# Attention in front of two expert layers: query parts stacked on the partitions, two score products per head instead of three

## The chip, the cores and the metric

The kernel runs on one core of a Trainium2 chip as a single program. The metric is the device time of that program in microseconds, from launch to the last output; of several runs the median counts. The engines of the core have their own in-order instruction streams: TensorE (PE, with its weight loads shown apart as PEld), VectorE (DVE), ScalarE (ACT), GpSimd (POOL) and SyncE (SP, which here only issues DMAs).

## The reference

Attention over 4 sequences of 576 tokens, 8 heads of 64 elements, causal with a window of 128 and a linear bias per head, in float32. Its output (2304 tokens by 512) then goes through two layers of 8 experts each. Only the attention is touched here.

```python
scores = scale * np.matmul(q, k.transpose(0, 1, 3, 2))
mask = (rel >= 0) & (rel < window)                    # rel = i - j, window = 128
scores = np.where(mask, scores + bias[None], -1000000000.0)
attn = np.exp(scores - np.max(scores, axis=-1, keepdims=True))
attn = attn / (np.sum(attn, axis=-1, keepdims=True) + 1e-09)
attn_out = np.matmul(attn, v)
x = attn_out.transpose(0, 2, 1, 3).reshape(B * S, H * D)
x = _moe_ref(x=x, **moe_kwargs)
return _moe2_ref(x=x, **moe2_kwargs)
```

## The kernel before, in words

**Blocks and units.** A sequence is cut into four blocks of 128 tokens and a tail of 64 (`NB` = 4, `TL` = 64). The 4 sequences give 20 blocks. A block is worked off in four units, one for each pair of heads (`hp`). A unit computes the scores of 128 queries of both heads against the keys of the block and of the block before it (`qk`: 256 columns a head), adds the bias and finds the row minimum on DVE (L196), takes the exponent on ACT (L200), turns the result on PE (`trans`), copies it back to SBUF on ACT and DVE (L229 to L233), and multiplies it with v on PE (`pv`, L255). The loop at the end of the attention keeps `trans` two units and `pv` four units behind `qk`. At `hp` 1 and 3 it prepares the keys and the queries of the block after next (`prep_k`, `prep_q`): four PE transposes each into one of two shared PSUM tiles `pT`, and from there to SBUF.

**The score product.** PE multiplies in a rounded 32-bit format (`F32R`). To keep float32 accuracy, q and k are each split into a high part (what ACT's copy rounds to) and a low part (what DVE's subtraction leaves). A unit's score of one head is the sum of three products: qh·kh, ql·kh, qh·kl (L193, L194). The two heads of a pair lie on partitions 0 to 63 and 64 to 127 of the key tiles `kt`; the query tiles `qt` hold zeros on the partitions of the other head, which are written once at the start (`clear_qt`, L111 on ACT, L115 on POOL). The first block of each sequence is computed in plain float32 (`qf`, `kf`, L190), which PE issues as two passes; the tail block has both heads of a pair in one product (L209, three products in F32R).

**What sets the order.** The Python loop gives the program order; a scheduler of the framework then places the instructions of each engine, and semaphores are put where tiles meet. The SP queue issues the loads (L72) about three blocks ahead and the writes of finished rows (`x_dram<-xr`, L313) in one in-order stream. POOL makes the distance table `rel` (L87 to L90) from which DVE makes the eight bias tables `bm` (L119), ahead of the first scores. After the attention the routing of the first expert layer begins, which needs the gate values of all tokens.

## Time and profile before

| | us |
|---|---|
| median of 3 runs (1073.11, 1077.97, 1077.48) | 1077.48 |
| the profiled execution | 1077.98 |
| its span, first to last instruction | 1076.1 |
| TensorE busy over the span | 947.7 (88%) |
| VectorE busy | 590.5 (55%) |
| ScalarE busy | 387.8 (36%) |
| GpSimd busy | 331.6 (31%) |
| mean granted TensorE clock | 0.93 |

The profiled execution is 1.9 us longer than its span and 0.5 us longer than the median of the runs. Busy shares over the whole span mix the attention (the first 180 us or so), the routing between the layers, and the expert products. For this change only the attention's stretch matters, and in it the views by time window and the timeline. PE's instructions overlap, so the duration shown of one matmul is longer than the step from one to the next; the step is read from the starts of the weight loads.

### The profile page before, as it was taken

The page shows a single profiled execution, that of the slowest core. Times are in us where ns is not written, and L with a number is a line of the kernel's source. Part 1 is how long each engine was busy: PE and PEld are TensorE (multiplying, and loading weights), DVE is VectorE, ACT ScalarE, POOL GpSimd, SP SyncE. Part 2 cuts the span into 40 slices and gives each one's busy share as a digit, 9 for nine tenths or more (in the row PEclk, how much of TensorE's full clock was granted, in tenths as well). Part 3 has the DMA queues.
Part 4 walks back from the last instruction along what each step waited for, and adds up shares of the span by engine and source line. Part 5 has one row for each costly group of instructions (what it writes and reads, how often), then busy time and mean ns, then how long its engine had stood idle before and what let it go on. Part 6 is the DMA issues. An engine that isn't in the chain of part 4 may idle for free. (4 is left out here: it accounts for less than half of the span.)

```text
span 1076.1 us, 18169 instructions
## 1 busy us (share of the span) xinstructions
PE 947.7 (88%) x6625; PEld 851.7 (79%) x6626; DVE 590.5 (55%) x1842; ACT 387.8 (36%) x793; POOL 331.6 (31%) x449
## 2 busy tenths in 40 slices
PE   8999998699999999989689698795995986959995
PEld 7999997488888799988579587685885886858894
DVE  8777686776797796878327153351531533515320
ACT  7777773223243264545115032221321322213210
POOL 9524421111100111032454417146153171461102
PEclk9999998599999999999799699898996998989998
DMA  9869621465443455545136144162351441623202
GB/s 203 204 145 211 162 66 55 149 206 170 148 154 108 125 168 167 179 122 181 46 59 186 35 108 134 46 137 76 89 132 30 108 133 46 134 79 90 32 11 35
DMA packets 114748, 125.66 MB, mean 117 GB/s; under 512 B 68128, under 2 KB 77344, under 8 KB 114656
## 3 DMA queue, kind: packets, MB, share of 16 engines
q1 hardware_dynamic: 98384, 90.93, 29.4%
q0 software_dynamic: 16272, 33.54, 14.6%
q8 instruction: 53, 0.87, 0.3%
q14 instruction: 39, 0.32, 0.1%
HBM read 100.69 MB, written 24.53 MB: 116 GB/s over the span
## 5 line engine op out<-in xcount | busy, mean ns | idle before, releaser
L899 PE MATMUL psG<-xh,w 128*128 128x312 f32 (+3 forms) x1536 | 362.0, 321 | 80.6 <-DVE hl L923 42.0
L899 PEld LDWEIGHTS psG<-xh,w 128*128 128x128 f32 x1536 | 273.4, 201 | 90.2 <-DVE hl L923 47.9
L899 PE MATMUL psG<-xl,w 128*128 128x312 f32 (+3 forms) x768 | 243.8, 318 | 3.3 <-issue 3.3
L923 DVE SCALAR_TENSOR_TENSOR hl<-psG,hh 128x312 fp32r<-128x312 f32 (+3 forms) x160 | 74.7, 475 | 247.4 <-ACT hh L922 169.9
L1334 PE MATMUL psG<-w,hh 128*128 128x512 f32 (+1 forms) x640 | 204.2, 396 | 0.1
L1224 POOL DMA_INDIRECT xrow<-x_dram,sr x156 | 153.2, 982 | 139.2 <-DVE sz L1041 63.2
L922 ACT ACTIVATE hh<-psG 128x312 fp32r<-128x312 f32 (+3 forms) x160 | 66.6, 426 | 307.3 <-PE psG L899 178.1
L899 PEld LDWEIGHTS psG<-xl,w 128*128 128x128 f32 x768 | 154.8, 202 | 3.0 <-issue 2.4
L1367 POOL DMA_INDIRECT out_dram<-y,sx x40 | 68.1, 1702 | 279.2 <-DVE y L1366 277.9
L1334 PEld LDWEIGHTS psG<-w,hh 128*128 128x128 f32 (+1 forms) x640 | 118.6, 185 | 30.5 <-DVE hl L923 0.6
L767 DVE TENSOR_TENSOR w<-raw,w 128x1024 fp32r<-128x1024 f32 x108 | 129.9, 1214 | 20.4 <-ACT w L766 17.2
L766 ACT ACTIVATE w<-raw 128x1024 fp32r<-128x1024 f32 x108 | 110.2, 1054 | 78.4 <-PE psG L1334 70.0
L1334 PE MATMUL psG<-w,hl 128*128 128x512 f32 (+1 forms) x320 | 126.4, 395 | 0.0
L749 POOL DMA_INDIRECT xg<-x_dram,ix x24 | 25.8, 1075 | 193.9 <-DVE w L426 54.1
L956 PE MATMUL psG<-hf,w2f 128*128 128x288 f32 x256 | 73.0, 426 | 0.0
L1366 DVE TENSOR_SCALAR y<-psG,sw 128x512 f32<-128x512 f32 (+1 forms) x40 | 29.7, 743 | 76.1 <-PE psG L1334 75.0
L1334 PEld LDWEIGHTS psG<-w,hl 128*128 128x128 f32 (+1 forms) x320 | 59.4, 185 | 14.6
L960 PE MATMUL psG<-hh,w 128*128 128x288 f32 x256 | 56.1, 305 | 3.9 <-ACT hh L922 3.9
L255 PE MATMUL pO<-v,pt 128*128 128x65 f32 x448 | 58.8, 269 | 0.3
L329 POOL DMA_DIRECT2D xq<-x_dram x60 | 33.0, 557 | 83.8 <-DVE rc L276 29.3
L200 ACT ACTIVATE pr<-tt,nm 128x256 f32<-128x256 f32 (+1 forms) x128 | 55.2, 474 | 6.2 <-DVE nm L196 5.6
L255 PEld LDWEIGHTS pO<-v,pt 128*128 128x128 f32 x448 | 55.9, 191 | 1.2 <-ACT pt L229 0.8
(297 smaller groups left out, 1302.2 us busy)
## 6 DMA issues: line engine op xcount, KB each, us to landing
raw<-in_moe_w_dram SPq DMA_DIRECT2D x112, 512.0 KB
w2f<-in_moe_w_dram SPq DMA_DIRECT2D x16, 512.0 KB
x_dram<-xr SPq DMA_DIRECT2D x18, 264.0 KB
out_dram<-zero POOLq DMA_DIRECT2D x18, 256.0 KB
x_dram<-x2r SPq DMA_DIRECT2D x96, 48.0 KB
rawk<-in_k_dram SPq DMA_DIRECT2D x16, 256.0 KB
rawq<-in_q_dram SPq DMA_DIRECT2D x16, 256.0 KB
v<-in_v_dram SPq DMA_DIRECT2D x16, 256.0 KB
```

Of the source, the lines that this page charges most:

```text
L200: nc.scalar.activation(pr[:, s, j0:], tt[:, s, j0:], AF.Exp, bias=nm[:, s:s + 1], scale=-1.0)
L255: nc.tensor.matmul(o[:, hh + s, :], pt[:, s, j, :], (vp, vc)[j][:, 2 * hp + s, :], start=j == js[0], stop=j == 1)
L766: nc.scalar.activation(h, t, AF.Copy)
L767: nc.vector.tensor_tensor(l, t, h.bitcast(F32), op=OP.subtract)
L899: nc.tensor.matmul(pg[:, :n], w1[a][kd][:, f * P:(f + 1) * P], XX[b][:, kd, cols], start=k_ == 0, stop=k_ == 3 * KD - 1)
L922: nc.scalar.activation(hh[:, f, cols], pg, AF.Relu)
L923: RELU[0] = nc.vector.scalar_tensor_tensor(hl[:, f, cols], pg, 0.0, hh[:, f, cols].bitcast(F32), op0=OP.max, op1=OP.subtract)
L956: nc.tensor.matmul(pg[:, :CAP], W2F[n, f // 2][:, f % 2, d * P:(d + 1) * P], hf[n % 2][:, f, :], start=f == 0, stop=f == KF - 1)
L960: nc.tensor.matmul(pg[:, :CAP], w2[a][f // 2][:, f % 2, d * P:(d + 1) * P], HH[b][:, f, cols], start=f == 0 and k_ == 0, stop=f == KF - 1 ...
L1224: nc.gpsimd.indirect_dma_start(out=t[:, u * P:(u + 1) * P], out_offset=None, in_=src, in_offset=bass.IndirectOffsetOnAxis(ap=SRC[e, j][u], ...
L1334: nc.tensor.matmul(py[:m], HH[b][:, f, j * P:j * P + m], w2[a][f // 2][:, f % 2, :], start=k_ == 0, stop=k_ == 3 * KF - 1)
L1367: x = nc.gpsimd.indirect_dma_start(out=out[:, :], out_offset=bass.IndirectOffsetOnAxis(ap=IDX[e, j][:n], axis=0), in_=y, in_offset=None, b ...
```

## The change

Each head gets its own stacked operands. The query tile of a block now holds, for head s of a pair, the high part on that head's 64 partitions and the low part on the other 64 (instead of zeros there). The key tile `kd[s]` holds the high part of head s on both halves, and `kz[s]` the low part on the head's half and zeros on the other. Then qt·kd gives qh·kh + ql·kh in one product, and qt·kz gives qh·kl: two products a head.

For this `prep_k` writes, for each of the four full blocks and each head: the high part (ACT, 64 partitions), the low part (DVE, 64 partitions), and the high part again on the other half: in the first sequence by ACT for head 0 and by DVE for head 1, in the other three by a DMA from SBUF to SBUF on the SP queue. The zeros of `kz` are written once by POOL. The tail block goes to plain float32: `kft` holds the last 192 keys, `qtt` the queries, and one product takes the place of three; the tail's low parts are no longer made. The zeros in `qt` and their clearing on ACT and POOL are gone.

```diff
-        kt = [[ap_.tile([P, NP, KW], F32R, name=f"kt{j}{i}") for i in range(2)] for j in range(NBUF)]
-        qt = [[ap_.tile([P, NP, 2, P], F32R, name=f"qt{j}{i}") for i in range(2)] for j in range(3)]
+        kd = [[ap_.tile([P, NP, NB * P], F32R, name=f"kd{j}{s}") for s in range(2)] for j in range(NBUF)]
+        kz = [[ap_.tile([P, NP, NB * P], F32R, name=f"kz{j}{s}") for s in range(2)] for j in range(NBUF)]
+        qt = [ap_.tile([P, NP, 2, P], F32R, name=f"qt{j}") for j in range(3)]
...
+        kft = [ap_.tile([P, NP, P + TL], F32, name=f"kft{j}") for j in range(2)]
+        qtt = [ap_.tile([P, NP, 2, TL], F32, name=f"qtt{j}") for j in range(2)]
...
         def clear_kt(j):
-            for i in range(2):
-                nc.gpsimd.memset(kt[j][i][:, :, S:].bitcast(F32), 0.0)
+            for s in range(2):
+                nc.gpsimd.memset(kz[j][s][half(1 - s)].bitcast(F32), 0.0)
...
-        clear_qt(qt[0], "a")
-        clear_qt(qt[1], "p")
+        clear_kt(0)
...
-            nc.scalar.activation(kh[:, :, sl], pk[:, :, :n], AF.Copy)
-            nc.vector.tensor_tensor(kl[:, :, sl], pk[:, :, :n], kh[:, :, sl].bitcast(F32), op=OP.subtract)
+            if i >= NB - 1:
+                nc.scalar.activation(kft[b % 2][:, :, (i - NB + 1) * P:(i - NB + 1) * P + n], pk[:, :, :n], AF.Copy)
+            if i == NB:
+                return
+            sl = slice(i * P, i * P + n)
+            for s in range(2):
+                r, o = half(s), half(1 - s)
+                h, z = kd[b % NBUF][s], kz[b % NBUF][s]
+                nc.scalar.activation(h[r, :, sl], pk[r], AF.Copy)
+                nc.vector.tensor_tensor(z[r, :, sl], pk[r], h[r, :, sl].bitcast(F32), op=OP.subtract)
+                if b > 0:
+                    nc.sync.dma_start(h[o, :, sl].bitcast(F32), h[r, :, sl].bitcast(F32))
+                elif s:
+                    nc.vector.tensor_copy(h[o, :, sl], pk[r])
+                else:
+                    nc.scalar.activation(h[o, :, sl], pk[r], AF.Copy)
...
+                nc.scalar.activation(t[r, :, s, :], pq[r], AF.Copy, scale=-0.125)
+                nc.vector.scalar_tensor_tensor(t[o, :, s, :], pq[r], -0.125, t[r, :, s, :].bitcast(F32),
+                                               op0=OP.mult, op1=OP.subtract)
...
-                    for n_, (x, y) in enumerate(((qh, kh), (ql, kh), (qh, kl))):
-                        nc.tensor.matmul(s_ps[:, s, :], x[:, hp, s, :], y[:, hp, w], start=n_ == 0, stop=n_ == 2)
+                    for n_, y in enumerate((kd, kz)):
+                        nc.tensor.matmul(s_ps[:, s, :], qtile(b, i)[:, hp, s, :], y[b % NBUF][s][:, hp, w],
+                                         start=n_ == 0, stop=n_ == 1)
...
-                for n_, (x, y) in enumerate(((qh, kh), (ql, kh), (qh, kl))):
-                    nc.tensor.matmul(s_ps[:, 0, :], x[:, hp].rearrange("p a b -> p (a b)"), y[:, hp, w],
-                                     start=n_ == 0, stop=n_ == 2)
+                nc.tensor.matmul(s_ps[:, 0, :n], qtt[b % 2][:, hp].rearrange("p a b -> p (a b)"), kft[b % 2][:, hp, :],
+                                 start=True, stop=True)
```

The change also moves instructions, since the scheduler places them anew. Three places are shown. Line numbers in rows of the changed kernel are its own, up to 16 higher than before.

ACT, from its first copy of keys on. Before (kt is the high part of the keys, qf the first block's queries, L200 the exponents of a unit):

```order
L152 ACTIVATE kf_119<-pT 128x512
L153 ACTIVATE kt_107<-pT 128x4x128
L168 ACTIVATE qf_117<-pT 64x4x128 x2
L200 ACTIVATE pr<-tt,nm 128x128 x2
L153 ACTIVATE kt_107<-pT 128x4x128
L200 ACTIVATE pr<-tt,nm 128x128 x2
L173 ACTIVATE qt_111<-pT 64x4x128
L229 ACTIVATE pt<-pP 128x2x128
L200 ACTIVATE pr<-tt,nm 128x128
```

The same place after (L161 is the high part on a head's own half, L168 its copy to the other half, L213 the exponents):

```order
L152 ACTIVATE kf_120<-pT 128x512
L161 ACTIVATE kd_107<-pT 64x4x128
L182 ACTIVATE qf_118<-pT 64x4x128 x2
L168 ACTIVATE kd_107<-pT 64x4x128
L161 ACTIVATE kd_108<-pT 64x4x128
L213 ACTIVATE pr<-tt,nm 128x128 x2
L161 ACTIVATE kd_107<-pT 64x4x128
L240 ACTIVATE pt<-pP 128x2x128
L168 ACTIVATE kd_107<-pT 64x4x128
L161 ACTIVATE kd_108<-pT 64x4x128
L213 ACTIVATE pr<-tt,nm 128x128 x2
```

Ahead of the first exponents there now stand two more copies, and in the built program the first of them (L168) waits for DVE, which reads the same PSUM tile just before it.

DVE, from the bias tables on. Before (L154 is the low part of the keys, L196 a unit's bias and minimum):

```order
L119 TENSOR_SCALAR bm<-rel 128x256 x8
L154 TENSOR_TENSOR kt_108<-pT,kt_107 128x4x128
L196 ISA tt,nm<-pS,bm 128x128
L196 ISA nm 128x1
L196 ISA tt,nm<-pS,bm 128x128
```

After (L162 is the low part of one head's keys, L166 the copy of head 1 to the other half, L138 a tail table):

```order
L125 TENSOR_SCALAR bm<-rel 128x256 x8
L162 TENSOR_TENSOR kz_111<-pT,kd_107 64x4x128
L138 TENSOR_SCALAR bmt<-relt,slt 128x192
L209 ISA tt,nm<-pS,bm 128x128
L209 ISA nm 128x1
L209 ISA tt,nm<-pS,bm 128x128
L209 ISA nm 128x1
L162 TENSOR_TENSOR kz_112<-pT,kd_108 64x4x128
L166 CAST kd_108<-pT 64x4x128
L162 TENSOR_TENSOR kz_111<-pT,kd_107 64x4x128
```

The first subtraction still stands behind all eight bias tables, and the first unit's rows are now followed by two subtractions and a copy.

SP, where the keys of the second sequence are prepared, after (kd is a copy from SBUF to SBUF; before, the same stream has the loads and the writes of `x_dram` alone):

```order
L71 DMA rawk<-in_k_dram 128x8x64
L324 DMA x_dram<-xr 128x528
L164 DMA kd_109<-kd_109 64x4x128
L71 DMA rawq<-in_q_dram 128x8x64
L164 DMA kd_110<-kd_110 64x4x128
L71 DMA v_76<-in_v_dram 128x8x64
```

The copies stand between loads that are issued about three blocks ahead, and behind the write of a finished block.

## Rows read from the trace of the kernel before

**Rows 1.** Busy time by windows of 27 us: PE, PEld, DVE, ACT, POOL, clock, DMA

```profile
core 0: us, PE busy (x) PEld busy (x) DVE busy (x) ACT busy (x) POOL busy (x), PEclk, DMA share, GB/s
27.00:54.00 27.00, 27.00 (x234) 25.79 (x234) 19.65 (x89) 20.16 (x54) 15.28 (x44) 1.00 0.88 205
```

**Rows 2.** Busy time by shorter windows, the start and the end of the attention

```profile
12.00:15.00 3.00, 2.98 (x23) 2.62 (x23) 2.94 (x12) 2.93 (x9) 2.99 (x10) 1.00 0.64 88
15.00:18.00 3.00, 2.81 (x24) 2.44 (x23) 2.44 (x10) 2.25 (x6) 3.00 (x11) 1.00 1.09 267
18.00:21.00 3.00, 3.00 (x29) 2.86 (x27) 2.81 (x13) 2.62 (x7) 3.00 (x7) 1.00 1.14 317
...
180.00:185.00 5.00, 2.88 (x26) 2.49 (x26) 1.81 (x14) 0.60 (x1) 0.14 (x1) 0.62 0.14 54
```

**Rows 3.** Timeline of weight loads, a full block: start us, us, engine, line, tiles

```profile
59.47 0.77 PEld L194 LDWEIGHTS pS<-kt,qt 128*128 128x128 f32 x6
60.19 0.46 PEld L227 LDWEIGHTS pP<-ident,pr 128*128 128x128 f32 x4
60.62 0.77 PEld L194 LDWEIGHTS pS<-kt,qt 128*128 128x128 f32 x6
...
64.20 0.97 PEld L346 LDWEIGHTS pT<-wgq,xt 128*128 128x128 f32 x8
65.09 0.78 PEld L194 LDWEIGHTS pS<-kt,qt 128*128 128x128 f32 x6
```

**Rows 4.** Timeline of weight loads, a unit of a tail block

```profile
81.11 0.42 PEld L209 LDWEIGHTS pS<-kt,qtt 128*128 128x128 f32 x3
...
81.46 0.97 PEld L255 LDWEIGHTS pO<-v,pt 128*128 128x128 f32 x8
```

**Rows 5.** Timeline of PE, plain float32 products of 288 columns (expert layer)

```profile
227.45 2.59 PE L956 MATMUL psG<-hf,w2f 128*128 128x288 f32 x10
```

**Rows 6.** The same line's instructions: duration ns min/median/max

```profile
L956 PE MATMUL psG<-hf,w2f x256: 403/406/687, 227.4 to 365.9; 128*128 128x288 f32 x128
```

**Rows 7.** Groups by form to 165 us: shapes, count, busy us, mean ns, idle before

```profile
L173 ACT ACTIVATE qt<-pT 64x512 fp32r<-64x512 f32 x24 | 14.2, 591 | 0.4
...
L154 DVE TENSOR_TENSOR kt<-pT,kt 128x512 fp32r<-128x512 f32 x16 | 11.0, 686 | 2.2 <-ACT kt L153 2.1
...
L153 ACT ACTIVATE kt<-pT 128x512 fp32r<-128x512 f32 x16 | 9.5, 593 | 2.7 <-PE pT L147 2.6
...
L174 DVE SCALAR_TENSOR_TENSOR qtt<-pT,qtt 64x256 fp32r<-64x256 f32 x8 | 3.3, 418 | 2.1 <-ACT qtt L173 1.9
```

**Rows 8.** Timeline of the start: bias tables, first key split, first exponents

```profile
1.98 0.94 POOL L115 MEMSET qt<- 128x1024 f32 x1
...
3.75 5.26 DVE L119 TENSOR_SCALAR bm<-rel 128x256 f32<-128x256 f32 x8 [0.24 <-POOL rel L90]
...
6.48 1.21 ACT L168 ACTIVATE qf<-pT 64x512 f32<-64x512 f32 x2
...
8.93 0.68 DVE L154 TENSOR_TENSOR kt<-pT,kt 128x512 fp32r<-128x512 f32 x1
...
9.85 0.69 ACT L200 ACTIVATE pr<-tt,nm 128x128 f32<-128x128 f32 x2 [2.16 <-DVE nm L196]
```

**Rows 9.** Timeline of ACT, the first exponents of a full block

```profile
17.77 0.91 ACT L200 ACTIVATE pr<-tt,nm 128x256 f32<-128x256 f32 x2
```

**Rows 10.** Timeline, a write of finished rows and the read that waits for it

```profile
24.01 0.93 SPq L313 DMA_DIRECT2D x_dram<-xr  x1
```

**Rows 11.** Timeline of POOL, that read

```profile
28.66 2.25 POOL L329 DMA_DIRECT2D xq<-x_dram  x4 [0.73 <-DMA x_dram<-xr]
```

**Rows 12.** Timeline, first and last piece of one query split

```profile
54.66 0.59 ACT L173 ACTIVATE qt<-pT 64x512 fp32r<-64x512 f32 x1
...
57.09 0.69 DVE L174 SCALAR_TENSOR_TENSOR qt<-pT,qt 64x512 fp32r<-64x512 f32 x1
```

More of the change, by code (lines that the diff above doesn't have):

```diff
@@ L96, with half @@
         NBUF = 2
-        kt = [[ap_.tile([P, NP, KW], F32R, name=f"kt{j}{i}") for i in range(2)] for j in range(NBUF)]
-        qt = [[ap_.tile([P, NP, 2, P], F32R, name=f"qt{j}{i}") for i in range(2)] for j in range(3)]
+        kd = [[ap_.tile([P, NP, NB * P], F32R, name=f"kd{j}{s}") for s in range(2)] for j in range(NBUF)]
+        kz = [[ap_.tile([P, NP, NB * P], F32R, name=f"kz{j}{s}") for s in range(2)] for j in range(NBUF)]
+        qt = [ap_.tile([P, NP, 2, P], F32R, name=f"qt{j}") for j in range(3)]
         qf = [ap_.tile([P, NP, 2, P], F32, name=f"qf{j}") for j in range(2)]
         kf = [ap_.tile([P, NP, P], F32, name=f"kf{j}") for j in range(2)]
-        qtt = [[ap_.tile([P, NP, 2, TL], F32R, name=f"qtt{j}{i}") for i in range(2)] for j in range(2)]
+        kft = [ap_.tile([P, NP, P + TL], F32, name=f"kft{j}") for j in range(2)]
+        qtt = [ap_.tile([P, NP, 2, TL], F32, name=f"qtt{j}") for j in range(2)]
+        def half(s):
+            return slice(s * 64, s * 64 + 64)
         def clear_kt(j):
-            for i in range(2):
-                nc.gpsimd.memset(kt[j][i][:, :, S:].bitcast(F32), 0.0)
+            for s in range(2):
+                nc.gpsimd.memset(kz[j][s][half(1 - s)].bitcast(F32), 0.0)
         def clear_qt(t, eng):
@@ L135, in tail_tables @@
                 nc.vector.tensor_scalar(bmt[:, hp, :], relt, slt[:, hp:hp + 1], None, op0=OP.mult)
-            clear_qt(qtt[0], "p")
-            clear_qt(qtt[1], "p")
+            clear_qt(qtt, "p")
             clear_qt(qf[1:], "p")
@@ L148, in prep_k @@
                     "p a d -> p (a d)"), ident[:n, :n])
-            kh, kl = kt[b % NBUF]
-            sl = slice(i * P, i * P + n)
             if i == 0:
                 nc.scalar.activation(kf[b % 2], pk, AF.Copy)
-            nc.scalar.activation(kh[:, :, sl], pk[:, :, :n], AF.Copy)
-            nc.vector.tensor_tensor(kl[:, :, sl], pk[:, :, :n], kh[:, :, sl].bitcast(F32), op=OP.subtract)
+            if i >= NB - 1:
[14 more added lines that the diff above has]
+                    nc.scalar.activation(h[o, :, sl], pk[r], AF.Copy)
         def qtile(b, i):
-            return qt[(b * (NB - 1) + i - 1) % len(qt)] if i < NB else qtt[b % 2]
+            return qt[(b * (NB - 1) + i - 1) % len(qt)]
         def prep_q(b, i):
@@ L164, in prep_q @@
                     "p a d -> p (a d)"), ident[:n, :n])
-            if i == 0:
+            if i in (0, NB):
+                t = (qtt if i else qf)[b % 2]
                 for s in range(2):
-                    r = slice(s * 64, s * 64 + 64)
-                    nc.scalar.activation(qf[b % 2][r, :, s, :], pq[r], AF.Copy, scale=-0.125)
+                    nc.scalar.activation(t[half(s), :, s, :], pq[half(s), :, :n], AF.Copy, scale=-0.125)
                 return
-            qh, ql = qtile(b, i)
+            t = qtile(b, i)
             for s in range(2):
-                r = slice(s * 64, s * 64 + 64)
-                nc.scalar.activation(qh[r, :, s, :n], pq[r, :, :n], AF.Copy, scale=-0.125)
-                nc.vector.scalar_tensor_tensor(ql[r, :, s, :n], pq[r, :, :n], -0.125,
-                                               qh[r, :, s, :n].bitcast(F32), op0=OP.mult, op1=OP.subtract)
+                r, o = half(s), half(1 - s)
+                nc.scalar.activation(t[r, :, s, :], pq[r], AF.Copy, scale=-0.125)
+                nc.vector.scalar_tensor_tensor(t[o, :, s, :], pq[r], -0.125, t[r, :, s, :].bitcast(F32),
+                                               op0=OP.mult, op1=OP.subtract)
         st = {}
         def qk(b, i, hp):
-            kh, kl = kt[b % NBUF]
             w = slice((i - 1) * P, (i + 1) * P)
```

5 lines of the change are left out of this document (removed).

## The prediction

> **What bounds the kernel now.** I read the busy time by windows first, then the timeline of the weight loads, then the start. The reader is to see three things. First, in the middle of the attention PE is busy in the whole window, 27.00 of 27.00 us, at full clock, with 234 instructions, while DVE is at 73% (19.65) and ACT at 75% (20.16) [rows 1]. A busy PE could still hide slack, so second: the steps. Six score products of 256 columns start within 60.19 - 59.47 = 0.72 us, 0.120 us each; four transposes within 60.62 - 60.19 = 0.43 us, 0.108 each; eight gate products, which have only 8 columns, within 65.09 - 64.20 = 0.89 us, 0.111 each [rows 3]. So PE goes from one instruction to the next without a pause, at about 0.11 us whatever the width, and 234 of them at 0.115 fill the window. Each PE instruction taken away there is worth its step. Third, the first 18 us are another regime: DVE is busy 2.94 of 3.00 us and ACT 2.93 in the window from 12 us, and PE issues only 23 to 24 instructions in 3 us instead of 29 [rows 2]. There DVE and ACT, not PE, set the pace. From 18 us on PE is full until the attention ends, shortly ahead of the window at 180 us, where its clock is at 0.62 [rows 2]. That is 160 us for four sequences less their start, about 40 us a sequence.
>
> **What PE saves.** Three full blocks in each of four sequences have split scores (the first block is plain float32): 12 blocks x 4 units x 2 heads = 96 products fewer, at 0.120 us, 11.5 us. The tail's three products take 81.46 - 81.11 = 0.35 us [rows 4]; now there are two float32 passes of 192 columns. The nearest row for a pass is 288 columns: ten of them in 2.59 us, of which the last has its duration of 0.403, so nine steps of 0.243 [rows 5, 6]; by columns, 192/288 of that is 0.162, two passes 0.324. 16 units x 0.026 = 0.4 us. Its ends are 0 gained and, if a pass cost no more than the 0.111 of a narrow one, 16 x 0.13 = 2.1. Together 11.9 us if PE stays the bound throughout.
>
> The Trainium skill (TensorE: Matmul & The Clock Gate, LDWEIGHTS) prices a weight load by its 128 columns, 107 ns, whatever is multiplied; our 0.108 to 0.111 agree, and by that rule alone the tail would gain the 2.1 us. The 0.243 of rows 5 say that a wide float32 pass costs more than its load, so the sum goes by columns.
>
> **What ACT and DVE get.** A copy of 64 partitions costs as much as one of 128: 591 against 593 ns [rows 7]. So a key tile's two halves double its cost. Per full block ACT gets one more copy and DVE one more subtraction; in the first sequence each also gets a copy to the other half. One such instruction is 0.6 us from start to start (1.21 for two on ACT; DVE's 686 ns less an overlap of about 0.09) [rows 7, 8]. The fourth block adds one `kft` copy, the tail's takes the place of the old one. DVE loses three half-length instructions of about 0.33 us (418 ns less the overlap) a sequence.
>
> **The start, step by step.** (a) POOL's clearing of `kz` stands where that of `qt` stood, ahead of the last step of `rel`; it is 2048 elements a partition instead of 1024, so 1.88 instead of 0.94 us, and the bias tables that wait for POOL begin at 4.7 instead of 3.75 and end at about 9.9 [rows 8]. (b) Behind them DVE subtracts the first keys (0.6, to 10.5); only then may ACT copy them to the other half, and the second head's copy is next: 2 x 0.6, to 11.7. Behind these two, in order, wait the first exponents, which before began at 9.85 [rows 8]: 1.85 us late, and PE's transposes and v products wait for them. (c) From there to the first exponents of a full block at 17.77 [rows 9] the key tiles of two more blocks are prepared: 2 x 2 more ACT instructions and one `kft`, 5 x 0.6 = 3.0 us, of which ACT's idle time in these windows, 0.07 + 0.75, takes 0.8 [rows 2]. Net 2.2, in all 4.05 us late. DVE's sum for the same stretch: (a) 0.94 and six more instructions, 3.6, less its 0.6 idle, 3.9, so neither engine can make up for the other. Ends: 0.94 (all of (b) and (c) beside other work) and 6 (nothing beside). ACT's old clearing of `qt` goes too, but it ran while ACT waited for the first keys: worth nothing. (d) The fourth key tile adds 1.2 us to ACT and to DVE while both are busy 2.62 and 2.81 of 3.00 [rows 2]. So the 16 products saved in the first sequence's first two split blocks bring nothing, and I add 0.5 us (ends 0 and 1.2).
>
> **The other three sequences.** Per 40 us ACT had about 30 and gets 4 x 0.6 + 0.6 = 3.0 more; DVE had 29 and gets 2.4 - 1.0 = 1.4 more; PE needs 37. That is 89% and 83% beside a full PE, so PE stays the bound on average, but the two run in order and with less room. At 75% PE showed no pause to speak of [rows 1]; I take 0.5 us a sequence, 1.5 in all. Ends: 0, and one instruction of 0.6 us exposed per key tile, 12 x 0.6 = 7.2.
>
> The 24 copies by DMA: behind each on SP stand loads, issued three blocks ahead, and the write of a finished block; they wait for ACT's copy, which comes a block and more ahead of those loads' use. The nearest row for the landing is a write of 264 KB, twice the size: issued at 24.01, and the read that waits for it goes at 28.66, so at most 4.65 us [rows 10, 11]. The keys are used seven units later, some 14 us. I cost them at nothing; what hides them is that lead. The DMA engines are at 0.88 in this stretch [rows 1], so a slower landing is possible, three times as slow is not likely.
>
> **Sum.** 80 products left at 0.120, 9.6, and the tail's 0.4 make 10.0 us; less 4.05, 0.5 and 1.5 leaves 3.95 us. The profiled execution took 1077.98 us, 0.5 above the median of the runs and 1.9 above its span, which the change does not touch; the routing behind the attention starts that much earlier and is otherwise the same. 1077.98 - 3.95 = **1074.0 us**.
>
> **Rivals.**
> - The start is hidden: only (a) is lost, PE keeps everything else, 11.9 - 0.94 = 11 us, **1067**. For it: PE also has idle time early that later work could fill. Against it: ACT and DVE are full from 12 us, and ACT's second copy waits for DVE by name. 0.22.
> - Slower: the key tile holds its PSUM tile too long. A query split goes ACT, DVE, ACT, DVE and takes 57.09 + 0.69 - 54.66 = 3.1 us [rows 12]; a key split took 0.593 + 0.686 = 1.3 [rows 7] and now has the same four steps. There are two `pT` tiles for all transposes, and PE, in order, waits at the next ones. The 1.8 us more on 16 key tiles are 29 us if all of it falls on PE; with half of it, 14.4 - 5.4 = 9 us slower, **1087**. It decides from 5.4/16 = 0.34 us a tile on. For it: PE shows no such margin. Against it: query splits do this in every block now, and PE is full. 0.10.
> - The clock falls at the start. By my steps PE has some 41 instructions between 12.6 and 21.5 us, 4.6 a us; in the window at 180 us it had 26 in 5 us, 5.2 a us, and the clock was granted at 0.62, between its levels of 2.4 and 1.2 GHz [rows 2]. At the lower level each would cost 0.11 us more, up to 4.5 in all: **1078.5**. Against it: those windows lie behind a PE that ran dry. The Trainium skill (TensorE: Matmul & The Clock Gate, Loop structure matters more than you think) says that the nest's spacing of matmuls decides whether they stay warm; the row at 180 us agrees. 0.12.
> - A float32 pass of 192 columns costs one narrow step: 1.7 us more gained, **1072.3**. The weight load rule above says so, rows 5 speak against it. 0.06.
> - The DMA copies land late, say 1 us of wait in each of 12 blocks: 12 - 4 = 8 slower, **1086**. 0.03.
> - My forecast, 1074, within 1071 to 1077: 0.47.
>
> **How the numbers follow.** About 0.5%, 5.4 us, is what a measurement of this kernel can tell from no change. Faster by more (below 1072.1): the first rival, half of the float32 one, and the near edge of the forecast, 0.22 + 0.03 + 0.09 = 0.34. Slower by more (above 1082.9): most of the PSUM and DMA rivals, 0.12. The rest, 0.54, is within. The range 1066 to 1082 leaves out the lower part of the first rival and the two slower ones, together about 0.2; it takes in the ends of the start (0.94 to 6) and most of those of the steady part.
>
> **What would show it.** In the changed profile: the first exponents of 128 columns near 11.7 us and the first of 256 near 21.8; ACT and DVE nearly full to about 25 us with PE below 29 instructions in 3 us; then PE full again with two weight loads a head, ACT near 89%; the tail's two passes at about 0.32 us; no PE wait for a DMA of `kd`; the end of the attention about 4 us earlier. I am wrong if the first 256-column exponents come before 19 us (then it is faster), if the clock is below 1.00 ahead of 30 us, or if PE in the later sequences stands waiting for ACT or DVE at key or query transposes (then it is slower).

## Result and profile after

The changed kernel takes 1085.66 us (median of 10 runs, 1080.18 to 1090.66), the kernel before on the same chip 1073.16 us (10 runs, 1069.23 to 1077.97). The ratio is 1.0121 with an interval of [1.0095, 1.0146]: 12.5 us slower. The prediction was 1074.0 us, 3.95 us faster than the profiled execution before, with a range of 1066 to 1082; it was wrong in size and in sign. The profiled execution after took 1089.15 us with a span of 1087.2.

The loss lies in the attention. The last finished rows of it (VectorE's last `xr`) end at 192.5 us; before they ended at 180.7, 11.8 us earlier. The order of the expert layers behind it is the same in both kernels.

Busy time by windows after; columns as in [rows 1]:

```profile
core 0: us, PE busy (x) PEld busy (x) DVE busy (x) ACT busy (x) POOL busy (x), PEclk, DMA share, GB/s
12.00:15.00 3.00, 2.48 (x12) 2.35 (x12) 2.97 (x11) 2.48 (x7) 2.95 (x2) 1.00 0.78 118
15.00:18.00 3.00, 2.18 (x10) 1.52 (x9) 2.91 (x5) 1.36 (x4) 2.99 (x11) 1.00 1.30 237
24.00:27.00 3.00, 1.97 (x8) 1.60 (x8) 2.34 (x8) 1.19 (x2) 3.00 (x2) 0.60 0.37 60
27.00:54.00 27.00, 26.77 (x221) 26.08 (x221) 21.23 (x84) 24.12 (x61) 10.78 (x34) 0.92 0.64 138
108.00:135.00 27.00, 25.38 (x200) 24.64 (x200) 19.44 (x80) 19.74 (x49) 10.49 (x28) 0.87 0.78 188
```

At the start VectorE is as full as in [rows 2], but from 15 us on it finishes 5 instructions in 3 us instead of 10, ScalarE falls to 1.36 of 3.00 us, and PE issues 10 to 12 instead of 23 to 24. Later PE has fewer instructions in the same time (200 to 221 instead of the 234 of [rows 1]; the change itself takes some away) and the clock is below 1.00. The 1.00 in the first two rows says nothing: the trace of the changed kernel holds no clock ahead of 21.2 us. Four weight loads of L266 took 0.93 us at 12.65 us and 0.52 us at 21.92, so these loads put PE at the lower of its two levels until then.

Two stretches show where. First the start, timeline of VectorE (start us, us, engine, line, tiles; in brackets idle time and what ended it):

```profile
4.92 4.06 DVE L125 TENSOR_SCALAR bm<-rel 128x256 f32<-128x256 f32 x8 [2.20 <-POOL rel L89]
...
13.72 1.97 DVE L138 TENSOR_SCALAR bmt<-relt,slt 128x192 f32<-128x192 f32 x1
...
18.28 0.31 DVE L138 TENSOR_SCALAR bmt<-relt,slt 128x192 f32<-128x192 f32 x1
20.38 2.32 DVE L138 TENSOR_SCALAR bmt<-relt,slt 128x192 f32<-128x192 f32 x1
```

The same stretch on GpSimd:

```profile
2.11 2.31 POOL L111 MEMSET kz<- 64x2048 f32 x1
4.49 0.40 POOL L89 TENSOR_SCALAR_AFFINE_SELECT rel<-rel 128x256 f32<-128x256 f32 x1
...
11.91 3.66 POOL L111 MEMSET kz<- 64x2048 f32 x2
...
19.57 1.55 POOL L460 IOTA jrow<- 128x256 bf16 x1
21.05 1.53 POOL L460 IOTA jone<- 128x256 bf16 x1
```

Two of the four tail tables (`bmt`) take 1.97 and 2.32 us instead of 0.31. The first ends at 15.69, when GpSimd's filling of `kz` ends (11.91 + 3.66 = 15.57); the second at 22.70, when its `jone` ends (22.58). So VectorE stands until GpSimd's work ends. Before, the four took 1.11 us together. The same stand was in the trace of before, hidden in the sum of eight `bm` tables in [rows 8] (duration in ns, min/median/max):

```profile
L119 DVE TENSOR_SCALAR bm<-rel x8: 274/424/3216, 3.8 to 8.7; 128x256 f32<-128x256 f32 x8
```

The first of them took 3.22 us, to 6.97, beside GpSimd's fillings of `qt` and `kt` from 3.67 us on; the others took 0.27 to 0.47.

ScalarE at the start:

```profile
9.61 0.59 ACT L168 ACTIVATE kd<-pT 64x512 fp32r<-64x512 f32 x1 [2.10 <-DVE kz L162]
...
10.83 0.69 ACT L213 ACTIVATE pr<-tt,nm 128x128 f32<-128x128 f32 x2
...
18.31 0.59 ACT L161 ACTIVATE kd<-pT 64x512 fp32r<-64x512 f32 x1 [1.95 <-PE pT L149]
...
25.76 0.60 ACT L154 ACTIVATE kft<-pT 128x512 f32<-128x512 f32 x1 [3.15 <-PE pT L149]
...
27.00 1.31 ACT L213 ACTIVATE pr<-tt,nm 128x256 f32<-128x256 f32 x3
```

The first exponents come at 10.83 instead of 9.85 [rows 8], the first of 256 columns at 27.00 instead of 17.77 [rows 9]. Most of the 9.2 us arise between the two.

Second, the change of sequence. Weight loads where the third sequence begins:

```profile
108.31 0.22 PEld L238 LDWEIGHTS pP<-ident,pr 128*128 128x128 f32 x1
110.35 0.18 PEld L238 LDWEIGHTS pP<-ident,pr 128*128 128x128 f32 x1 [1.81 <-ACT pr L213]
110.36 1.03 PEld L266 LDWEIGHTS pO<-v,pt 128*128 128x128 f32 x4
111.16 0.33 PEld L238 LDWEIGHTS pP<-ident,pr 128*128 128x128 f32 x1
```

And ScalarE there:

```profile
107.42 0.39 ACT L240 ACTIVATE pt<-pP 128x256 f32<-128x256 f32 x1
108.77 0.39 ACT L240 ACTIVATE pt<-pP 128x256 f32<-128x256 f32 x1 [0.96 <-PE pP L238]
109.18 0.59 ACT L187 ACTIVATE qt<-pT 64x512 fp32r<-64x512 f32 x1
109.80 0.51 ACT L213 ACTIVATE pr<-tt,nm 128x256 f32<-128x256 f32 x1
```

It is a round trip: ScalarE waits 0.96 us in order for a transpose of PE, then has a query copy (L187) ahead of the exponents (L213), and PE stands 1.81 us for those. From 109.9 us, while PE stood, to 116.7 us the granted clock is 0.50: four loads of L266 take 1.03 us there, 0.53 at 104.86 us. So what PE waited for there are the exponents, and not a key or query transpose.

### The profile page after: what moved, and what is told of

Same layout as the page of the kernel before. It is cut to its first block, busy times and chain, and to the rows that moved or that the text cites. A ratio compares the mean times of both kernels' runs of the same rounds, so it can differ in the third digit from the quotient of the medians.

```text
span 1087.2 us, 18047 instructions
## 1 busy us (share of the span) xinstructions
PE 951.1 (87%) x6514; PEld 852.4 (78%) x6514; DVE 603.5 (56%) x1850; ACT 398.6 (37%) x815; POOL 331.4 (30%) x443
## 5 line engine op out<-in xcount | busy, mean ns | idle before, releaser
L910 PE MATMUL psG<-xh,w 128*128 128x312 f32 (+3 forms) x1536 | 362.4, 322 | 80.7 <-DVE hl L934 57.9
L760 POOL DMA_INDIRECT xg<-x_dram,ix x24 | 25.6, 1066 | 195.8 <-DVE w L437 54.4
L266 PE MATMUL pO<-v,pt 128*128 128x65 f32 x448 | 61.4, 273 | 1.6 <-DVE xr L294 1.0
L266 PEld LDWEIGHTS pO<-v,pt 128*128 128x128 f32 x448 | 59.3, 197 | 2.8 <-POOL qf L121 0.9
L213 ACT ACTIVATE pr<-tt,nm 128x256 f32<-128x256 f32 (+1 forms) x128 | 55.1, 475 | 3.2 <-DVE nm L209 2.6
```

The lines of the kernel that those rows point to most:

```text
L213: nc.scalar.activation(pr[:, s, j0:], tt[:, s, j0:], AF.Exp, bias=nm[:, s:s + 1], scale=-1.0)
L266: nc.tensor.matmul(o[:, hh + s, :], pt[:, s, j, :], (vp, vc)[j][:, 2 * hp + s, :], start=j == js[0], stop=j == 1)
L910: nc.tensor.matmul(pg[:, :n], w1[a][kd][:, f * P:(f + 1) * P], XX[b][:, kd, cols], start=k_ == 0, stop=k_ == 3 * KD - 1)
```

## Experiments

Each ratio is to the kernel before, run on the same chip. The table also gives, from one trace each, the end of VectorE's last `xr` of a block: before in us, the others as the difference. One trace is one execution; where it and the ratio disagree, the ratio counts.

| kernel | ratio [interval] | block 1 | seq. 1 | seq. 2 | seq. 3 | seq. 4 |
|---|---|---|---|---|---|---|
| before | 1 | 23.4 | 57.1 | 99.2 | 142.1 | 180.7 |
| changed | 1.0121 [1.0095, 1.0146] | +10.6 | +9.5 | +10.0 | +12.3 | +11.8 |
| e1_third | 1.0117 [1.0082, 1.0151] | +10.2 | +10.7 | +11.3 | +12.2 | +12.7 |
| e2_before_two | 0.9988 [0.9960, 1.0016] | -0.2 | -2.0 | -2.0 | -4.7 | -4.7 |
| e3_dma_all | 1.0196 [1.0164, 1.0229] | +0.5 | +15.6 | +16.1 | +17.3 | +20.3 |
| e4_bmt_pool | 1.0068 [1.0042, 1.0094] | +7.4 | +6.8 | +6.7 | +7.9 | +8.0 |
| e5_lag | 1.0078 [1.0048, 1.0108] | +9.6 | +9.2 | +9.1 | +7.5 | +5.4 |
| e6_two_lag | 0.9946 [0.9917, 0.9974] | +1.2 | +1.1 | -0.7 | -1.6 | -4.5 |
| e7_before_lag | 0.9987 [0.9964, 1.0009] | +2.0 | +1.8 | +1.9 | +1.9 | +0.4 |
| e8_defer | 1.0073 [1.0048, 1.0098] | +7.5 | +6.9 | +9.4 | +10.3 | +8.9 |
| e11_single0 | 1.0122 [1.0084, 1.0160] | +1.9 | +2.9 | +5.3 | +7.6 | +11.3 |
| e9_plain0 | 1.0159 [1.0106, 1.0212] | -1.1 | +11.7 | +12.3 | +15.0 | +15.4 |
| e10_plain0_lag | 1.0114 [1.0070, 1.0158] | +6.6 | +11.7 | +12.1 | +12.6 | +9.7 |
| e12_no_lock | 1.0144 [1.0088, 1.0200] | -2.6 | +7.1 | +9.9 | +13.3 | +13.5 |
| e13_no_lock_lag | 1.0139 [1.0086, 1.0193] | -1.4 | +9.2 | +9.6 | +14.5 | +19.9 |
| e14_single0_third | 1.0152 [1.0107, 1.0198] | +2.5 | +4.3 | +8.6 | +10.7 | +12.0 |
| e15_fill | 1.0155 [1.0136, 1.0173] | +10.2 | +9.3 | +9.9 | +10.8 | +12.5 |
| e16_const_pool | 1.0111 [1.0075, 1.0148] | -1.3 | +2.8 | +5.5 | +8.3 | +8.9 |
| e17_const_fill | 1.0094 [1.0072, 1.0116] | -2.4 | +0.7 | +1.1 | +1.5 | +1.9 |
| e18_fill_lag | 1.0107 [1.0078, 1.0137] | -1.3 | +4.0 | +3.3 | +8.0 | +7.2 |

In the runs e12 to e18 the kernel before takes 955 to 958 us. The part behind the attention is some 112 us shorter there (in e14 777 us from the last `xr` to the end of the span, in e11 889, at a granted clock of 0.97 and 0.92 over the whole span); why, no run shows. There is no trace of the kernel before from these runs, so their rows in the table are set against the one from the longer runs (e15's first block ends where e1's does, at +10.2). One per cent is 9.6 us there.

**Products or preparation?** e1 puts a third, unused product back into the changed kernel:

```diff
+                    nc.tensor.matmul(s_ps[:, s, :], qtile(b, i)[:, hp, s, :], kd[b % NBUF][s][:, hp, w],
+                                     start=True, stop=True)
                     for n_, y in enumerate((kd, kz)):
```

> The changed kernel with a third score product put back per head (the first product is computed twice, the first result is overwritten; the output is unchanged). PE's work per unit is as before the change, all preparation as after. Theory A: in the changed kernel PE is no longer the bound; it stands waiting for ACT and DVE and its clock falls in between, so 96 more products of 0.12 us fill waits: within 3 us of the changed kernel (ratio to the kernel before 1.009 to 1.015), perhaps a little faster if the clock stays up. Theory B: the whole loss is in the start and PE still sets the pace from 40 us on: 80 x 0.12 = 9.6 us slower than the changed kernel, ratio to before about 1.021.

e2 takes the third product out of the kernel before:

```diff
-                    for n_, (x, y) in enumerate(((qh, kh), (ql, kh), (qh, kl))):
-                        nc.tensor.matmul(s_ps[:, s, :], x[:, hp, s, :], y[:, hp, w], start=n_ == 0, stop=n_ == 2)
+                    for n_, (x, y) in enumerate(((qh, kh), (ql, kh))):
+                        nc.tensor.matmul(s_ps[:, s, :], x[:, hp, s, :], y[:, hp, w], start=n_ == 0, stop=n_ == 1)
```

> The kernel before without the third product of the full blocks (the term high q times low k is left out; everything is still prepared as before). This is the saving on PE alone, with none of the change's preparation. If PE is the bound from 18 us on, as the prediction's sum has it: 96 x 0.12 = 11.5 us less a little of the start, 9 to 11.5 us faster than before (ratio 0.989 to 0.992). Rival: the round trips through ACT and DVE pace the units as soon as PE has less to do, or the clock falls: 0 to 4 us faster (ratio above 0.996).

With the changed kernel this is a table of two by two. Three products, old preparation: 1. Two, old: 0.9988. Three, new: 1.0117. Two, new: 1.0121. The 96 products are worth 1.3 us with the old preparation (interval 4.3 gained to 1.7 lost) and nothing with the new; the preparation costs 12.6 us with three products and some 14 with two. This alone refutes the sum of the prediction.

e2's expectation named two reasons why the products might not come out, the round trips and the clock. Its window from 60 to 180 us (the attention ends at 176.0):

```profile
60.00:180.00 120.00, 116.58 (x989) 110.22 (x988) 86.92 (x399) 83.16 (x223) 39.12 (x103) 0.98 0.55 134
```

In this trace 4.7 us of the 11.5 come out, more than the medians show. From 18 to 176 us PE is idle 2.9 us more than before, 2.1 of it behind 142 us. The clock is at half from 57.9 to 61.3 us, which at half speed costs 1.7 us (an estimate), so the clock alone does not hold the products. That leaves some 2 us without a place.

**DMA instead of the engines in the first sequence.** e3:

```diff
-                if b > 0:
+                if b >= 0:
                     nc.sync.dma_start(h[o, :, sl].bitcast(F32), h[r, :, sl].bitcast(F32))
```

> The changed kernel with the keys of the first sequence doubled by DMA too, as in the other three. Takes 4 copies each from ACT and DVE and shortens the chain in which they alternate on one PSUM tile. Theory: the chain is what delays the start, so the first exponents of a full block come 3 to 5 us earlier (near 23 instead of 27.0) and the time falls by 3 to 5 us (ratio to before 1.007 to 1.009). Rival: the DMA engines are full in the first 24 us (share above 1.0), the copies land late behind the loads and PE waits for them: no gain or slower than the changed kernel.

Without the copies on the engines the first block is only 0.5 us late, but the first exponents of 256 columns come at 32.73 instead of 27.00, and the first sequence ends 15.6 us late. The time is as the rival said, but late copies are the smaller part of it. PE waits once for a copy, 2.03 us up to 22.82; the long stand has VectorE at its end (timelines of VectorE and of the weight loads):

```profile
23.78 3.99 DVE L467 TENSOR_SCALAR tri<-jp 128x128 bf16<-128x128 f32 x1
...
33.03 0.29 PEld L206 LDWEIGHTS pS<-kd,qt 128*128 128x128 f32 x1 [9.20 <-DVE nm L209]
```

Five small tables for the routing, `tri` the first, keep VectorE from 23.78 us until the next key split at 28.94, most of it while GpSimd fills two large tables (23.35 to 27.31), and behind them stand the splits of keys and queries and the rows that PE waits for. So e3 does not price the copies by DMA; what they cost without that stand was not tried.

**VectorE behind GpSimd.** e4 gives the four tail tables to GpSimd:

```diff
-                nc.vector.tensor_scalar(bmt[:, hp, :], relt, slt[:, hp:hp + 1], None, op0=OP.mult)
+                nc.gpsimd.tensor_scalar(bmt[:, hp, :], relt, slt[:, hp:hp + 1], None, op0=OP.mult)
```

> The changed kernel with the four tail tables (bmt) multiplied on POOL instead of DVE. In the changed profile two of them took 1.97 and 2.32 us on DVE, as long as POOL's memset and table writes beside them lasted, against 0.32 for the others. Theory: DVE and POOL block each other there and this delays the key chain behind it; without it 3 to 4 us faster than the changed kernel (ratio to before 1.008 to 1.009). Rival: those two waits lie beside ACT's and PE's own waits and nothing is gained (ratio 1.012).

GpSimd needs 3.00 us for them (timeline of e4):

```profile
10.45 3.00 POOL L138 TENSOR_SCALAR bmt<-relt,slt 128x192 f32<-128x192 f32 x4
```

The time falls from 1.0121 to 1.0068 of before, about 5.7 us and more than the 3 to 4 expected (in the trace the attention ends 3.8 us earlier), and the first block by 3.2 us, near the 3.67 by which the two tables were too long. So a good part of the loss comes from a line that the change does not touch; it only moved it beside other work of GpSimd. The Trainium skill (SBUF — State Buffer, SBUF: two separate sides) describes such a wait: GpSimd and VectorE share a pair of ports, which one of them holds for a whole instruction. The ends at 15.69 and 22.70 agree with that.

**Lags.** e5 (on e4), e6 (on e2) and e7 (on before) keep the transposes three units and the v products five behind the scores (three further counters, not shown, go up by one as well):

```diff
-LB, LC, LG, LH = (2, 4, 6, 13)
+LB, LC, LG, LH = (3, 5, 7, 14)
```

> The changed kernel with the tail tables multiplied by GpSimd (1.0068 of before, about 1081 us), and now the transposes three units and the v products five units behind the scores (two and four so far; the gate steps one unit later as well). Theory R (round trips): in the later sequences TensorE waits because exponents and their transposes are only two units apart, so that each delay on ScalarE reaches it; one unit more hides it, the saved score products come out, and the time falls by 6 to 11 us, to 1070 to 1075. Rival W (work): ScalarE and VectorE are full with their own instructions and the fixed time between them; another order leaves 1081, or 1083 with the one unit more at the end.

> The kernel before without its third score product in the full blocks (the low part of the keys is left out of the scores; that kernel took as long as before, ratio 0.9988), and with the lags of three and five units. Theory R: the 96 products of 0.12 us now come out, 1063 to 1066. Rival W: as without the lags, 1074 to 1077.

> The kernel before with the lags of three and five units alone, the control of the two others. Theory R: TensorE was full with three products, so the order brings nothing and one unit more at the end costs up to 2 us: 1073 to 1077. Rival W: the same. If it is as much faster as the kernel with two products, the lag is worth something by itself and says nothing of the products.

With the old preparation and the lag the products are worth 4.4 us of 11.5 (0.9946 against 0.9987), between the two theories of e6; the lag alone changes nothing, as both said (e7). That the lag lets them out is not shown: the intervals of e6 and e2 overlap, and in the traces the attention ends 4.5 and 4.7 us early, the same with the lag and without. With the new preparation nothing comes out (1.0078 against 1.0068), as rival W said.

**The start, the order.** e8 (on e4) splits the first block's keys only behind the first unit's scores:

```diff
-        prep_k(*blocks[0])
+        prep_k(*blocks[0], when=0)
...
                 if n == K1:
+                    prep_k(*blocks[0], when=1)
                     prep_k(*blocks[1])
```

> The changed kernel with the tail tables by GpSimd, and the key split of the very first block put behind the first unit's scores in the program, so that the first exponents no longer stand behind the copies to the other half. Theory S (the order at the start): the first exponents come about 1 us earlier, the clock rises earlier, and of the 7 us that the first block is still late 2 to 4 go: 1077 to 1079. Rival: the work is only moved, and the first exponents of 256 columns, which need all of it, come at the same time: 1081.

No gain (1.0073, first block +7.5): the first exponents come at 9.22 us instead of 10.82, the first of 256 columns at 24.09 instead of 22.18, so the work was only moved, as the rival said. My step (b), two copies ahead of the first exponents, was not where the loss was.

**The start, the work.** e11 (on e4) splits the first sequence's keys as before:

```diff
+            if b == 0:
+                nc.scalar.activation(kd[0][0][:, :, sl], pk, AF.Copy)
+                nc.vector.tensor_tensor(kz[0][0][:, :, sl], pk, kd[0][0][:, :, sl].bitcast(F32), op=OP.subtract)
+                return
```

> The changed kernel with the tail tables by GpSimd (1.0068 of before), and in the first sequence alone the key split as before: one ScalarE copy and one VectorE subtraction of 128 partitions a block, no copies to the other half (the first sequence's scores then lack the doubled halves; both heads use one pair of key tiles). The other three sequences and all counts of products stay. Theory P (preparation): the six further instructions a block on ScalarE and VectorE are what is left of the loss at the start, so the first write of finished rows is issued near 24 to 26 us instead of 30.9 and the time falls by 5 to 7 us, ratio 0.999 to 1.003. Rival C (clock, order): TensorE's late clock and the order of the first exponents make the loss; then at most 2 us go, ratio near 1.006.

The first block is 1.9 us late instead of 7.4: the further instructions of the key split cost 5.5 us there, as theory P said (four a block by the edit, three on each engine instead of one, not six). But the time did not fall; it rose to 1.0122, outside both bands. In its trace the other three sequences lose 8.4 us, at each first block (+2.4, +3.0, +5.5), and the clock is at half for 20.9 us of them. A gain at the start was given back.

**A first sequence without a split.** e9 (on e4) computes it in plain float32, e10 adds the lags. Of e9's edit the products are shown; it also gives the first sequence a key tile of its own, `k0`, and single instead of double buffers to `kf`, `kft` and `qtt`, and moves the clearing of `kz` behind the tail tables. These went along into e10, e12, e13 and e16 to e18 and were not tried alone:

```diff
+                    if b == 0:
+                        qs = qf[i % 2][:, hp, s, :]
+                        nc.tensor.matmul(s_ps[:, s, j0:], qs, k0[:, hp, max(i - 1, 0) * P:(i + 1) * P],
+                                         start=True, stop=True)
+                        continue
```

> A version with the same outputs as the kernel before: as the changed kernel with the tail tables by GpSimd, but the first sequence has no split at all: its scores are plain float32 (two passes of TensorE a head), its keys need one ScalarE copy a block and its queries two, VectorE does no split there. Theory P: VectorE and ScalarE, which were full in the first 18 us, get room even against before; the first write of finished rows at 22 to 25 us, and the time is 3 us below to 1 us above before, 0.997 to 1.001. Rival C: two float32 passes of 256 columns at about 0.22 us each instead of two products of 0.12 cost 24 x 0.2 = 5 us of TensorE, and the start gains nothing: 1.007 to 1.011.

> The same with the lags of three and five units. Theory P with R (round trips): the start as before and about 4 us of the saved products in the other three sequences: 0.993 to 0.998, faster than before. Rival: with the lags it is as without them.

Both are slower than theory P's bands (1.0159 and 1.0114), and e9 than rival C's too. In e9 the first block comes 1.1 us ahead of before, and the second 8.5 us late. VectorE's timeline shows why:

```profile
24.27 5.61 DVE L483 TENSOR_SCALAR trim<-jp 128x128 bf16<-128x128 f32 x1
24.41 5.51 DVE L488 TENSOR_SCALAR ones<-ones,pcol 128x128 bf16<-128x128 bf16 x1
29.84 0.40 DVE L221 CUSTOM_DVE_ANT_0 tt<-pS,bm 128x256 f32<-128x256 f32 x1
```

Small tables for the routing, 0.2 us each elsewhere, stand 5.5 us, to 29.9 us, while GpSimd fills two large ones (24.47 to 28.47 us) and small ones right behind them. It is the stand that e3 showed. e12 makes these tables on GpSimd, e13 adds the lags, e16 moves one more (`quad`), whose input VectorE in e12 awaited from GpSimd for 6.6 us. One of the five lines of e12:

```diff
-    nc.vector.tensor_scalar(trim, jp, 0.5, -1.0, op0=OP.is_lt, op1=OP.mult)
+    nc.gpsimd.tensor_scalar(trim, jp, 0.5, -1.0, op0=OP.is_lt, op1=OP.mult)
```

> The version whose first sequence is plain float32 (1.0159 of before), with one edit: five small tables of the later routing (tri, upp, trim and two of ones) are made by GpSimd. In its trace VectorE stood in one of them for 5.5 us from 24.3 us on while GpSimd filled A and oh, and the second block, which had been 1.1 us ahead of before at the first, was 8.5 us late. Theory L (the two engines block each other): without them the first sequence ends at most 1 us behind before, the clock does not fall at 27 us, and the time falls by 8 to 12 us, ratio 1.003 to 1.008. Rival F (float32 passes): the first sequence is late because TensorE has more to do there; the time falls by under 3 us.

> The same with the lags of three and five units; its outputs are those of the kernel before. Theory L with R: the first sequence level with before and about 4 us of the saved products from the other three, ratio 0.994 to 0.999, faster than before. Rival: 1.005 or more, as the lagged version without the edit was 1.0114 and the tables matter little.

> The version whose first sequence is plain float32 and whose small tables are made by GpSimd (1.0144; its VectorE still stood 6.6 us from 27.3 us on, waiting for one more table, quad), with that table by GpSimd too. Theory L (VectorE behind GpSimd): its first sequence, 2.6 us ahead of before at the first block, stays at most 2 us behind at its end (it was 7.1), and the time falls by 4 to 7 us, 1.006 to 1.011. Rival F (float32 passes): the first sequence ends 5 us or more late, 1.012 or more.

e12 missed theory L's band (1.0144), as the stand taken away was followed by the next, and e13 with the lags came out as its rival said (1.0139). With the last one gone, e16's first sequence ends 2.8 us late instead of 9.5, on the edge of its band, and the ratio is 1.0111. The first sequence can thus be had for 2.8 us, and still the time is 1.1% above before: again the later sequences lose 6 us.

**Clock or engines?** e14 (on e11) puts the unused products back, as e1 did. e15 (on the changed kernel) puts eight unused transposes ahead of those for which PE waits at each new sequence, e17 (on e16) four, e18 adds the lags:

```diff
+            if i == 0 and b > 0:
+                for _ in range(8):
+                    nc.tensor.transpose(pp[:, 0, 0, :], ident, ident)
```

> The kernel with the first sequence's key split as before (1.0122 of before; its first sequence ended 2.9 us late and the others lost 8 us more, with 24 us at half clock between 60 and 161 us), with one product more a head in the split blocks, whose sum is started anew and so not used: 96 instructions of 0.12 us. Theory K (clock): fuller, TensorE keeps its clock in the later sequences, and in spite of 11.5 us more of work the time is the same or up to 6 us lower, ratio 1.006 to 1.013. Rival B (TensorE is the bound after all): 8 to 12 us slower, 1.020 or more.

> The changed kernel (1.0121 of before) with eight unused transposes of the identity ahead of the transposes of each first-block unit in the last three sequences: 96 instructions of 0.11 us, 10.6 us of TensorE, at the place where it stood for up to 1.8 us waiting for exponents and where the granted clock fell to one half in the next stretch. Theory K (clock): they run while TensorE would wait, the clock stays at full there, and the time is the same or up to 6 us lower, 1.006 to 1.013. Rival B (TensorE is the bound): 7 to 11 us more, 1.018 or more. Rival A (ScalarE and VectorE set the pace whatever the clock): no fall of the clock between 35 and 190 us and yet the same time, 1.010 to 1.014.

> The same with four unused transposes ahead of each of those first-block units, 48 instructions, 5.3 us. Theory K with L: 2 to 6 us below the version without them, 1.000 to 1.008. Rival B: 3 to 5 us above it.

> The version with the plain first sequence, all constant tables by GpSimd and four unused transposes ahead of each first-block unit (1.0094; its attention ended 1.9 us behind before in its trace and its clock stayed at full), with the lags of three and five units. Theory R with K: with the clock held the lag gives 2 to 4 us of the saved products back, the attention ends 0 to 3 us ahead of before, ratio 1.003 to 1.008. Rival: the lag worked only where TensorE was kept waiting; the same within 2 us, 1.007 to 1.011. Faster than before, under 0.998, would be a version that beats both; neither theory gives it.

Windows of the three later sequences (60 to 180 us), before:

```profile
60.00:180.00 120.00, 119.90 (x1036) 115.42 (x1035) 87.59 (x389) 85.12 (x224) 39.10 (x102) 1.00 0.55 132
```

The changed kernel:

```profile
60.00:180.00 120.00, 114.75 (x931) 108.22 (x929) 92.48 (x385) 93.18 (x238) 42.99 (x112) 0.96 0.68 167
```

e1, with the unused products:

```profile
60.00:180.00 120.00, 118.08 (x1001) 112.40 (x999) 93.96 (x387) 94.39 (x239) 42.61 (x111) 1.00 0.67 167
```

e15, with the unused transposes:

```profile
60.00:180.00 120.00, 119.88 (x1033) 114.94 (x1031) 94.16 (x388) 93.21 (x239) 42.45 (x111) 1.00 0.69 169
```

The rows of e16 and e17:

```profile
60.00:180.00 120.00, 116.38 (x913) 110.31 (x914) 89.60 (x371) 89.39 (x227) 42.56 (x111) 0.93 0.70 166
60.00:180.00 120.00, 117.34 (x993) 110.67 (x992) 92.70 (x383) 91.46 (x237) 42.45 (x111) 1.00 0.70 165
```

The changed kernel has 105 PE instructions fewer in 120 us than before, and gets no further. Filled up with 96 useless ones at its waits (e15), it has as many as before, keeps its clock at 1.00, and still gets no further: its last `xr` is 0.7 us behind that of the changed kernel, for 10.6 us of work. Rival B (PE is the bound) is out: with e14, 1.0152 [1.0107, 1.0198], and e15, 1.0155 [1.0136, 1.0173], 11 us of added work cost about 1.5 and 2.3 us by the ratios. (This takes it that e11's 13.1 and the changed kernel's 12.5 us, 1.013 there, are the same in the faster runs; neither was run there.) Theory K, that the clock swallows the saving, is not borne out either as the whole cause: e15's clock does not fall, and its time is above K's band. It lies nearest to rival A (1.014 at most, the interval begins at 1.0136), that the pace is set by ScalarE and VectorE and the round trips to them; no run takes work off these two in the later sequences, so that stays an argument. Between e16 and e17 the clock is held too, and the trace ends 7 us earlier; in the timed runs only 2.5 us lie between the medians, and the intervals overlap. In e18 the lag brings nothing, as its rival said, but its clock is not held either (0.97 from 60 to 180 us).

One order in the traces bears on the clock. From the end of the first sequence to the end of the attention e17 loses 1.2 us, e4 1.2, the changed kernel 2.3, e16 6.1 and e11 8.4; their clocks over 60 to 180 us are 1.00, 0.97, 0.96, 0.93 and 0.91, in the same order. (The other versions with two products and the old lags fit in roughly: e8 2.0 at 0.97, e9 3.7 at 0.97, e3 4.7 at 0.96, e12 6.4 at 0.94.) So where more is lost there, PE ran longer at half clock. e17 against e16 says that holding the clock gets most of it back, in one trace each. But in e1 and e15 a held clock brought the changed kernel nothing, with some 11 us of work added. So the clock has some part, whose size is open. No version here that computes the whole beats the kernel before.

## Why the prediction was wrong, step by step

- **The step that failed:** "Each PE instruction taken away there is worth its step." The windows showed PE full [rows 1, 3], and I took full for limiting. The test is to take the work away: e2 did, and 96 products of 0.120 us brought 1.3 us instead of 11.5. In its trace, too, less than half came out, 4.7 us, and the clock accounts for only 1.7. That PE and the round trips over VectorE and ScalarE were about equally long before is the likely reading, argued and not shown. A hint of it was in the waits of before, which I had not weighed (60 to 180 us; engine, line, what it waited for, us in total, times, longest):

```profile
ACT pt L231 <- PE pP L227: 15.3, 22, 1.5
```

  ScalarE, busy 85.12 us of 120 (71%), stood 22 times for PE's transposes. A full PE would give such waits as well; but in e2, with 96 products fewer, they are still 12.2 us, 20 times.
- **What PE saves.** The steps themselves were right: two weight loads a head at 0.12 us. The tail's two passes gained more than I said (0.27 from start to start instead of 0.35, forecast 0.324):

```profile
89.61 0.30 PEld L220 LDWEIGHTS pS<-kft,qtt 128*128 128x128 f32 x2
89.88 1.02 PEld L266 LDWEIGHTS pO<-v,pt 128*128 128x128 f32 x8
```

- **The sum in two parts.** The trace ends the attention 11.8 us late instead of 3.95 early, 15.75 us apart. At the end of the first block it was 10.6 us late instead of 4.05: 6.55 from the start. Behind it 1.2 us more were lost where 8.0 should have been gained: 9.2 from the rest of the attention, where the products did not come out.
- **The start** was mis-sized: 9.2 us at the first 256-column exponents instead of 4.05 (10.6 at the end of the first block). (a) did not come: `rel` was later, but the `bm` tables then took 4.06 us instead of 5.26 and ended at 8.98, where they had ended before (9.01). I had taken the 5.26 for work; 3.22 of it was the first table alone, standing beside GpSimd, and in both kernels that table ends at 6.97 us. (b) was 0.98 instead of 1.85. The rest, mostly (c), is at the end of the first block 5.5 us of copies (e11) and 3.2 us for the stand of the tail tables (e4), which I did not see coming; 1.9 us are left in e11. With that stand taken out, e4's first 256-column exponents come near the forecast of 21.8:

```profile
22.18 0.51 ACT L213 ACTIVATE pr<-tt,nm 128x256 f32<-128x256 f32 x1
```

  Up to there the sum was about right, 4.41 against 4.05, in part by luck: (a) fell out and (c) was some 3.4 instead of 2.2. The neighbour on GpSimd was missing. Nor did both engines stay nearly full to 25 us: ScalarE is at 1.36 of 3.00 us from 15 us on.
- **The clock at the start** (rival, 1078.5) is late as feared: first full at 21.2 us instead of 10.5, and at half again from 24.6 to 31.4. Yet e1's was full from 10.6 to 17.4 us and its first block was 10.2 us late: by itself it decides little.
- **The steady part** was 1.5 us of stalls in the forecast, and is as much as the saving and 1.2 us more. PE does wait in the later sequences, as I wrote it would if I was wrong, but not at key or query transposes: at the transposes of the exponents, where a sequence begins. The rival that gave 1087 (the key tile holds its PSUM tile) came near the number by luck and named another place: PE stands at key transposes for VectorE's copy (L166) once by name, 1.11 us up to 17.15 us, at the start.
- **The DMA copies** in the last three sequences are hidden as said: no PE wait for a DMA of `kd` is in the trace. Where the lead is missing, as in e3, PE waits for one of them once, 2.03 us.
- **The engines' shares** came out near: in 27 to 54 us ScalarE is at 24.12 of 27.00 us, 89%, VectorE at 79% (forecast 89% and 83%); over 60 to 180 us, where the pace is lower than forecast, they are at 78% and 77%.

What stays open: how the loss in the later sequences divides between the clock and the round trip, and why the clock falls longer in e11 and e16 than in e4. Taking ScalarE's query copy out of that chain was not tried.

## What to carry to other kernels

An engine that is busy all the time need not be the limit: if a second chain is as long, taking work off the first brings nothing, and the cheap test is to leave that work out. When a change adds copies to balance saved products, price them in the stretch where the receiving engines are full, and look at what the move brings side by side on GpSimd and VectorE, as lines that nobody edited may be what gets slow. In a row that sums several instructions, read the longest one as well as the sum.

## What was not expected of the hardware

- Some of VectorE's small operations from SBUF to SBUF stood until GpSimd's work beside them ended: 0.31 us becomes 1.97 and 2.32 (changed kernel), 0.2 us becomes 5.5 (e9), and one `bm` table took 3.22 us before the change. In the changed kernel VectorE's reads of PSUM beside GpSimd's filling of `kz` kept their durations (0.28 us for 128 columns, 0.68 for a subtraction).
- Two float32 passes of 192 columns took 0.27 us, less than by columns from the 288-column pass of [rows 5] (0.324).
